# First table's inputs and constants on SP's queue, and a new written order up to the second block's gate tiles, in an S4 convolution with a gated layer

## The chip, the cores and the metric

The kernel runs on one core of a Trainium2 chip. The core has a matrix engine (TensorE, PE in the profile, with PEld for its weight loads), a vector engine (DVE), a scalar engine for function tables (ACT), GpSimd (POOL) and a sync engine (SP) that here only issues DMAs. Every engine works through its own instructions in program order and waits for others by semaphores. DMAs are issued by SP, ACT or POOL, each with a queue of its own, and are moved by 16 DMA engines. The metric is device time in microseconds, the median of several executions.

## The reference

An input x of 2048 tokens by 448 channels passes two blocks, each with a layer norm and a modulation from a small vector c:

```python
x = A_u
mod = (silu(c) @ w_mod)                      # six rows of 448: sa, ca, ga, sb, cb, gb
h = layernorm(x) * (1 + ca) + sa
x = x + ga * conv(h)                         # S4 convolution, per channel
h = layernorm(x) * (1 + cb) + sb
x = x + gb * ((gelu(h @ w_gate) * (h @ w_up)) @ w_down)
```

The convolution's kernel is `K[d, l] = Re sum_n C[d,n] * exp(dt[d] * A[d,n] * l) * dt[d] * B[d,n]` for 256 complex states n and 2048 positions l, with `dt = exp(log_dt)`. `conv(h)` is the causal convolution of each channel of h with K (by FFTs of length 4096 in the reference) plus `h * Dskip`. The inner width of the gated layer is 1792.

## The kernel before, in words

The kernel is a list of 2006 tasks. Each has a name and a function that emits a few instructions; `PLACE` (lines 40 to 263) holds, for every name, one number for each of its tasks, and the tasks are emitted in the order of these numbers. A letter behind a number chooses the engine where there is a choice: a for ACT, d for DVE, p for POOL, s for SP. Since every engine runs its instructions in program order, `PLACE` is the order by which each engine and each DMA queue works. Costs that stand in the `add` calls are not read when the kernel is built.

**Start and tables.** The states' parameters come in four tables of 112 channels (`abc`, the function `prep`). For a table, two loads `p.ld` bring C, B and A; A1 and A2 form C times B on DVE; S1 to S4 on ACT and B1, D1, G1, E1 on DVE turn it into a log magnitude and a phase; C1, C2 and A3 scale A by dt. The results are cut into bf16 pieces: c0, d0, e0, f0 for the magnitudes, c1, d1, e1, f1 for the phases. `p.put0` and `p.put1` store them to the DRAM buffer `lh_d`, into which `pad` also copies two constant rows, and `lt0` and `lt1` load them back, transposed by the access pattern, as weights of matmuls, for 7 groups of 8 channels at a time. dt itself is made by the task `dt` from `c.ld`, and `silu` and `sil2` prepare c for the modulation.

Before the change the first table's two loads are issued by ACT, its pad by POOL, and everything else of the start by SP, beginning with a block of x (`x.ld`), which is followed by log_dt, c, and three blocks of w_mod (`m.ld`).

**Table phase.** For each of 56 groups of channels, PE makes exponents and angles (`x.mm`, `y.mm`, `ang`, `anc`) out of the weights and the constant tables `ea` and `rd` (`c.ea`, `c.rd`); ACT turns them into exponentials and sines (`x.exp`, `y.exp`, `sin`, `cos`), for some with an absolute value first (`mag`); DVE multiplies (`tx`, `tyc`); PE sums over the states (`kgen`). Two groups at a time, the result is taken out of PSUM (`kev`), gets Dskip (`kd`), is transformed by PE over 32 positions (`ka`) and copied out (`kout`).

Beside it the input is normed (`bn`, `norm`, and `as`, which scales a constant matrix by the tokens' deviation), transformed (`ua`, taken out by `ua.ev`, stored by `ua.st`) and brought to frequencies (`ub`, `ub.ev`, `ub.eg`, `ub.st`). For the channels up to 320, `f.fwd`, `f.pr`, `f.inv`, `f.z` and `f.st` transform K further, multiply by the input's spectrum, transform back and store the result `y`.

**Tail transforms.** The last 128 channels go through `t.fwd`, the products `t.p0` and `t.p1`, and two inverse transforms: `t.i0` for the rows that the first token block needs, through `t.z0`, a store `t.s0` to `yb_d` and loads `yi.l0` and `yi.l1`, and `t.inv` for the others, through `t.z` and `t.st`. The matrices come by `t.fc` (first part) and `t.fd` (second part, which only `t.inv` needs).

**Gated layer.** `co.mme` and `co.mml` sum the convolution's output for the first of four blocks of 512 tokens; residual and norm follow on DVE and ACT; `co.ta` and `co.tb` transpose the columns on PE. The gate and up matmuls (`gu2` in two halves for the first four tiles, then `gu`) and the down matmuls run block by block. The weights are split into f16 pairs on the chip (`w.le`, `w.la`, `w.ld` load them; `w.hi`, `w.lo`). `co.mmx`, a y load `yi.ld` and DMA transposes prepare the next block meanwhile.

How a task's number and letter become program order:

```python
        at = PLACE[n][i]
        self.at, e = int(at.rstrip("adps")), at[-1]
        self.on = {"a": "ACT", "d": "DVE", "p": "POOL", "s": "SP"}.get(e) or next(iter(eng))
...
        out = sorted(self.tasks, key=lambda t: t.at)
```

Lines of the profile: 511 and 514 are the first table's loads and pads, 542 is A1, 595 the stores of the pieces, 620 the loads of the weights, 638, 657 and 675 the exponent and angle matmuls, 721 and 725 the products, 748 `kgen`, 771 `ka`, 480 and 482 copies on ACT and DVE by a helper, 852 the loads of x, 805 those of w_mod, 1138 and 1140 `t.fc` and `t.fd`, 1189, 1207 and 1216 the tail's matmuls, 1224 and 1297 the stores and loads of `yb_d`, 1332 the weight loads, 1409 `co.mml`, 1470 the transposes, 1524 and 1530 the gate and up matmuls.

## Time and profile before

| | |
|---|---|
| median of 3 runs | 787.2 us (786.79 to 788.53) |
| the profiled execution, its own time | 788.84 us |
| its span, first to last instruction | 787.0 us |
| time outside the span | 1.84 us |
| PE busy | 728.1 us |
| DVE busy | 591.6 us |
| ACT busy | 459.5 us |
| moved by DMA | 139.87 MB |
| mean granted TensorE clock | 0.991 |

A row of the timeline has the start, the length, the engine, the line, the operation with its output and input, the count, and in brackets the idle time before it with what ended it. "SPq" and "ACTq" rows are DMAs being issued, not moved. A row of the groups has the count and, behind the bar, the busy time and the mean of one in ns, then the idle time of the engine ahead of them. A row of the stretches has the busy time of PE, PEld, DVE, ACT and POOL, the granted clock of TensorE, the busy share of the DMA engines and what they moved in GB/s. A row of the DMA issues ends with the size and the median time from issue to landing.

### The profile page before, as it was taken

The page shows a single profiled execution, that of the slowest core. Times are in us where ns is not written, and L with a number is a line of the kernel's source. Part 1 is how long each engine was busy: PE and PEld are TensorE (multiplying, and loading weights), DVE is VectorE, ACT ScalarE, POOL GpSimd, SP SyncE. Part 2 cuts the span into 40 slices and gives each one's busy share as a digit, 9 for nine tenths or more (in the row PEclk, how much of TensorE's full clock was granted, in tenths as well). Part 3 has the DMA queues.
Part 4 walks back from the last instruction along what each step waited for, and adds up shares of the span by engine and source line. Part 5 has one row for each costly group of instructions (what it writes and reads, how often), then busy time and mean ns, then how long its engine had stood idle before and what let it go on. Part 6 is the DMA issues. An engine that isn't in the chain of part 4 may idle for free.

```text
span 787.0 us, 19037 instructions
## 1 busy us (share of the span) xinstructions
PE 728.1 (93%) x8166; PEld 443.6 (56%) x8166; DVE 591.6 (75%) x893; ACT 459.5 (58%) x611; POOL 9.0 (1%) x24
## 2 busy tenths in 40 slices
PE   1786889998899999989999999999999999999998
PEld 0333454543667767768784445444595446944478
DVE  5989999999999999988768851469773587133743
ACT  4799999899999999961555640233421244012320
POOL 0000000000000000000300000000000000000000
PEclk9989899999999999999999999999999999999999
DMA  9654458997878767999697875345447324012201
GB/s 260 180 162 141 142 148 242 298 263 225 255 232 223 222 190 212 290 294 252 193 311 231 273 191 159 129 129 188 164 67 206 111 94 134 14 47 94 82 2 59
DMA packets 103790, 139.87 MB, mean 178 GB/s; under 512 B 34388, under 2 KB 85268, under 8 KB 103706
## 3 DMA queue, kind: packets, MB, share of 16 engines
q1 hardware_dynamic: 99940, 131.61, 57.0%
q10 hardware_dynamic: 3206, 6.07, 2.3%
q8 instruction: 64, 1.05, 0.6%
q0 software_dynamic: 560, 0.98, 0.4%
q14 instruction: 20, 0.16, 0.1%
HBM read 100.39 MB, written 36.01 MB: 173 GB/s over the span
## 4 chain that ended last, share of the span: by engine, by line
PE 69%; DVE 4%; ACT 4%; DMA 2%; issue 2%; SPq 1%; DVEq 0%; ACTq 0%
PE pq L1530 31%; PE pq L1630 9%; PE pf L1105 4%; PE pd L1599 4%; PE kg L748 4%; PE pf L1094 3%; PE pg L675 2%; PE pq L1524 2%; PE kg L771 2%; PE pd L1630 2%; DVE ty L725 1%; PE pd L1404 1%; PE pg L657 1%; ACT fg L692 1%; PE pf L1189 1%
## 5 line engine op out<-in xcount | busy, mean ns | idle before, releaser
L1530 PE MATMUL pq<-ht,wr 128*128 128x512 f16 (+1 forms) x1200 | 248.5, 365 | 1.3 <-DMA ht<-hl 1.2
L1530 PEld LDWEIGHTS <-wr 128*128 128x128 f16 x1200 | 114.5, 98 | 130.0 <-issue 13.0
L725 DVE TENSOR_TENSOR ty<-my,fg 128x2048 f32<-128x2048 f32 x56 | 127.5, 2283 | 0.8 <-issue 0.5
L1537 ACT ACTIVATE ge<-pq 128x512 f32<-128x512 f32 (+1 forms) x60 | 33.9, 565 | 102.1 <-PE pq L1524 68.7
L1544 DVE TENSOR_TENSOR fq<-ge,pq 128x512 f32<-128x512 f32 (+1 forms) x60 | 38.9, 649 | 71.5 <-PE pq L1530 44.3
L1556 ACT ACTIVATE hh<-fq 128x1024 f16<-128x1024 f32 (+1 forms) x49 | 46.7, 961 | 64.9 <-DVE fq L1544 46.4
L721 DVE TENSOR_TENSOR tx<-mx,fg 128x1024 f32<-128x1024 f32 x56 | 67.7, 1218 | 2.4 <-ACT fg L692 1.0
L1630 PE MATMUL pq<-d,hh 128*128 128x224 f16 x476 | 68.9, 259 | 0.0
L748 PE MATMUL kg<-ty,tx 128*32 128x64 f32 x3584 | 63.6, 222 | 4.7 <-issue 2.6
L748 PEld LDWEIGHTS kg<-ty,tx 128*32 128x32 f32 x3584 | 53.8, 111 | 23.8 <-issue 15.7
L1559 DVE TENSOR_TENSOR hlo<-fq,hh 128x1024 f16<-128x1024 f32 (+1 forms) x49 | 53.7, 1106 | 12.9 <-ACT hh L1556 12.7
L1630 PE MATMUL pq<-d,hlo 128*128 128x224 f16 x238 | 61.6, 259 | 0.0
L688 ACT ACTIVATE fg<-pg 128x1024 f32<-128x1024 f32 x56 | 58.0, 1038 | 1.2 <-PE pg L675 0.8
L662 ACT ACTIVATE my<-pg 128x1024 f32<-128x1024 f32 x56 | 55.5, 1031 | 2.0 <-PE pg L657 1.9
L1630 PEld LDWEIGHTS <-hh 128*128 128x128 f16 x560 | 54.1, 98 | 0.9 <-issue 0.2
L1105 PE MATMUL pf<-q,fc 128*128 128x160 f32 x264 | 41.5, 307 | 1.1 <-DVE q L1098 1.1
L692 ACT ACTIVATE fg<-fg,small 128x1024 f32<-128x1024 f32 x36 | 41.5, 1170 | 0.1
L1747 ACT ACTIVATE d<-fq 128x896 f16<-128x896 f32 x14 | 13.3, 947 | 46.1 <-PE pd L1599 27.3
L1105 PEld LDWEIGHTS pf<-q,fc 128*128 128x128 f32 x264 | 36.4, 190 | 6.5 <-issue 1.5
L675 PEld LDWEIGHTS <-lt 64*128 64x128 bf16 x304 | 18.0, 96 | 38.8 <-issue 26.5
L675 PE MATMUL pg<-ea,lt 64*128 64x512 bf16 x152 | 30.5, 392 | 7.6 <-ACT fg L699 3.4
L984 PE MATMUL pf<-ui,fu 128*128 128x448 f32 x66 | 31.0, 575 | 1.6 <-ACT uo L480 1.4
(210 smaller groups left out, 1117.6 us busy)
## 6 DMA issues: line engine op xcount, KB each, us to landing
wr<-w_d SPq DMA_DIRECT2D x21, 896.0 KB, 5.2
fc<-in_k_fc SPq DMA_DIRECT2D x20, 576.0 KB, 3.7
u_d<-so SPq DMA_DIRECT2D x32, 224.0 KB, 2.8
ui<-u_d SPq DMA_DIRECT2D x10, 672.0 KB
fq<-in_wd SPq DMA_DIRECT2D x14, 448.0 KB, 6.1
w<-in_wgu SPq DMA_DIRECT2D x11, 512.0 KB, 7.4
us<-uo SPq DMA_DIRECT2D x22, 240.0 KB, 5.2
q<-us SPq DMA_DIRECT2D x22, 240.0 KB, 6.4
```

What stands on the lines that cost most here:

```text
L662: A.activation(yb.tile.rearrange("p h (n k) -> p n h k", n=2), pb.tile.rearrange("p (n h k) -> p n h k", n=2, h=2), AF.Exp)
L675: T.matmul(pa[:, nh * 512:nh * 512 + 512], w, x, start=(k == 0), stop=(k == 2))
L688: A.activation(fb.tile[:, 0].rearrange("p x (n k) -> p n x k", n=2), pb.tile.rearrange("p (n x k) -> p n x k", n=2, x=2), AF.Sin, scale=TW ...
L692: A.activation(fb.tile[:, 1], fb.tile[:, 1], AF.Sin, scale=-TWO_PI, bias=halfpi)
L721: V.tensor_mul(tx.tile, xb.tile[:, xm, None, :].to_broadcast([128, 2, 512]), fb.tile[:, :, 0])
L725: V.tensor_mul(ty.tile, yb.tile[:, :, None, :].to_broadcast([128, 2, 2, 512]), fb.tile[:, None, :, 1].to_broadcast([128, 2, 2, 512]))
L748: T.matmul(kg[32 * g:32 * g + 32, 2 * (s % 2) + q, :64], tx[:, r, nh, 4 * q + g], ty[:, 0:4:3, nh, 4 * q + g] if r else ty[:, 1:3, nh, 4 * ...
L1105: T.matmul(pz.tile[:, e % 32 - sl0], fc.tile[:, i, 1 + t], pp.tile[:, t, i], start=(t == 0 and e != 32), stop=(t == 1 and e != 0))
L1530: T.matmul(pb.tile[k][:, ts], wr.tile[:, 4 * lo + t, k, c0:c0 + 128], ht[:, m, ts], start=f % 2 == 0 and i == 0, stop=f % 2 == 1 and i == 9)
L1556: A.activation(hg.tile[0][:, cb, c], fq.tile[:, c], AF.Copy)
L1559: V.tensor_sub(hg.tile[1][:, cb, c], fq.tile[:, c], hg.tile[0][:, cb, c])
L1630: T.matmul(bank(k)[:, m], x[:, p, q[0], ts], w[:, p, q[1]], start=new and m == 0 and p == 0 and z == 0, skip_group_check=True, stop=i in ( ...
```

## The change

Two things are changed. In `prep`, the two loads and the pad of the first table are issued by SP, as those of the other three tables were; ACT and POOL issue no DMA in the start any more. And `PLACE` has new numbers (and in part new letters) for every task up to number 1480; from there on all numbers are as before. The first table's first load is number 0 on SP, then come a block of x, the second load, c, a block of w_mod, log_dt, two more blocks of w_mod with a block of x between them, the pad, and the store of the first pieces. Some names have other letters. No task is added or removed. Of the table's rows only those that the text speaks of are shown.

```diff
--- before.py
+++ after.py
@@ -38,49 +38,49 @@
...
-    "as": "66d 64d 79d 107d 116d 151d 119d 185a 250d 258d 265a 289d 309d 333d 334d 365d",
+    "as": "69a 58a 101d 98d 121d 126d 174a 167d 251d 255a 280d 289a 311d 324d 334d 353a",
...
-    "c.c": "21",
+    "c.c": "16",
...
-    "c.ld": "11",
+    "c.ld": "21",
...
-    "c.rd": "58",
+    "c.rd": "78",
...
-    "co.ta": "1401 1406 1453 1436",
+    "co.ta": "1404 1410 1432 1434",
...
-    "co.tb": "1411 1413 1454 1439",
+    "co.tb": "1407 1414 1443 1446",
...
-    "dt": "12",
+    "dt": "24",
...
-    "f.fwd": "738 753 783 806 832 855 879 902 924 947 969 998 1014 1036 1055 1077 1098 1120 1141 1162 1209 1216",
+    "f.fwd": "727 759 786 809 821 850 884 892 930 950 966 998 1015 1028 1056 1075 1095 1120 1136 1160 1206 1218",
...
-    "f.z": "758a 778d 802a 829a 868a 871d 896d 926a 952d 979a 1005d 1019a 1038d 1061a 1085a 1102a 1128d 1143a 1163a 1188a "
-        "1235a 1239a",
+    "f.z": "755a 772d 812d 832a 865a 887d 908d 928a 949a 986d 993d 1009d 1027d 1066d 1085a 1098d 1111a 1132a 1155a 1183a "
+        "1219a 1233d",
...
-    "gu2": "1420 1427 1442 1457 1464 1467 1470 1473",
+    "gu2": "1422 1423 1442 1457 1459 1464 1471 1472",
...
-    "kev": "191d 238d 285d 351d 368d 401d 431d 497a 551d 579d 661a 680d 737d 786a 816a 856a 890d 922a 948d 980d 1045d 1065a "
-        "1104d 1146a 1183d 1198a 1219a 1246a",
+    "kev": "218d 224a 290d 317a 373d 394d 448a 490a 548d 569d 699d 707d 735d 806d 797d 858a 900a 918a 960d 975a 1037a 1071d "
+        "1101a 1138a 1166a 1195a 1235a 1238d",
...
-    "kout": "247a 288a 318a 377d 448a 414a 505a 530a 583d 634d 720d 733d 771a 811a 843a 892d 928a 962a 992a 993d 1076a 1110d "
-        "1142a 1177a 1200a 1228a 1251d 1252a",
+    "kout": "229a 266a 299d 342a 442d 407a 507a 544a 658a 598a 710a 738d 739a 843a 804a 877d 917a 945d 976a 994a 1070d 1094a "
+        "1130a 1167a 1188a 1211a 1244d 1246a",
...
-    "lt0": "65 149 317 358 568 766 860 955",
+    "lt0": "61 112 302 369 561 744 852 1017",
...
-    "lt1": "103 150 335 393 696 833 971 995",
+    "lt1": "95 162 384 432 742 745 965 1060",
...
-    "m.cp": "532d 589a 818d",
+    "m.cp": "553a 604a 793d",
...
-    "m.ld": "24 32 23 423 539 727",
+    "m.ld": "27 36 17 433 558 761",
...
-    "p.A3": "25 174 435 618",
+    "p.A3": "25 154 346 487",
...
-    "p.C1": "13 92 422 543",
+    "p.C1": "28 102 420 500",
...
-    "p.C2": "18 113 427 552",
+    "p.C2": "32 103 421 607",
...
-    "p.E1": "38 169 437 644",
+    "p.E1": "38 171 446 639",
...
-    "p.G1": "19 117 434 571",
+    "p.G1": "35 128 436 615",
...
-    "p.S1": "14 100 328 547",
+    "p.S1": "5 104 331 542",
...
-    "p.S2": "16 112 364 569",
+    "p.S2": "8 114 366 565",
...
-    "p.S3": "27 133 410 588",
+    "p.S3": "9 125 390 579",
...
-    "p.c0": "31a 194d 439a 662a",
+    "p.c0": "26a 159d 428d 632d",
...
-    "p.c1": "43d 183d 471a 682d",
+    "p.c1": "44a 241d 511a 729d",
...
-    "p.e1": "53a 217a 481a 692d",
+    "p.e1": "56d 321a 584d 845d",
...
-    "p.f0": "36 242 460 704",
+    "p.f0": "40 244 459 730",
...
-    "p.ld": "3 5 70 91 168 291 490 507",
+    "p.ld": "0 7 86 87 170 265 368 452",
...
-    "p.put0": "48 281 464 837",
+    "p.put0": "49 301 475 814",
...
-    "pad": "4 203 278 785",
+    "pad": "48 247 181 695",
...
-    "silu": "22",
+    "silu": "18",
...
-    "t.fd": "1256 1231 1244 1274 1221 1237 1215 1234",
+    "t.fd": "1180 1242 1266 1322 1227 1382 1376 1375",
...
-    "t.i0": "1269 1297 1296 1300 1310 1307 1314 1318 1334",
+    "t.i0": "1267 1274 1278 1307 1301 1311 1314 1331 1326",
...
-    "t.inv": "1272 1282 1290 1326 1354 1362 1376 1386 1395",
+    "t.inv": "1262 1315 1291 1350 1348 1359 1361 1406 1398",
...
-    "t.s0": "1315s 1304s 1309s 1313s 1319s 1330a 1322a 1333a 1342s",
+    "t.s0": "1300s 1318s 1289s 1310s 1309s 1319a 1320a 1336a 1328s",
...
-    "t.z0": "1280a 1301a 1298a 1305a 1316a 1311a 1320a 1324d 1337a",
+    "t.z0": "1273a 1297a 1288a 1308a 1306a 1312a 1316a 1332a 1327a",
...
-    "ua.ev": "78d 83a 88a 93d 110d 111d 120d 123d 141a 144a 156a 166d 188a 192d 231a 211a 259a 261a 267a 268a 299a 296a 303a "
-        "310d 325a 331a 344d 340a 366a 367d 375d 380d",
+    "ua.ev": "76d 74d 84d 88d 115d 111d 134d 130d 137a 148a 153a 155d 192d 185a 207a 215d 258a 256a 267a 270a 288a 284a 298a "
+        "305a 328a 329a 343d 336a 364d 362d 367d 372a",
...
-    "w.le": "1285 1344 1323",
+    "w.le": "1304 1290 1351",
...
-    "x.ld": "46 8 201 154",
+    "x.ld": "33 4 226 156",
...
-    "yi.l0": "1361s 1332s 1340p 1353p 1365s 1363p 1343p 1357p 1370p",
+    "yi.l0": "1369s 1360s 1335p 1367p 1345s 1337p 1354p 1371p 1368p",
...
-    "yi.l1": "1352s 1331p 1338a 1367p 1348s 1360p 1350p 1358s 1368s",
+    "yi.l1": "1357s 1373p 1313a 1365p 1358s 1340p 1362p 1372s 1363s",
...
@@ -508,12 +508,12 @@
         def ld1(i):
             if i == 0:
                 b1.tile = pq.tile([DT, 4, N], FT, name="q")
-            (dma if t else adma)(b3.tile[:, :2] if i else b1.tile, a["abc"][t, :, 4:] if i else a["abc"][t, :, :4])
-
-        L0 = add("p.ld", {"SP" if t else "ACT": 0.42 if t else 0.1}, v0, lambda: ld1(0), (), [b1], (), kb=459)
-        PAD[t] = add("pad", {"SP": 0.7} if t else {"POOL": 1.0}, v0 + 0.5, lambda: (dma if t else P.dma_start)(lh_d[t, :, :, 6:], a["k_one"][t]), [L0], kb=300)
+            dma(b3.tile[:, :2] if i else b1.tile, a["abc"][t, :, 4:] if i else a["abc"][t, :, :4])
+
+        L0 = add("p.ld", {"SP": 0.42}, v0, lambda: ld1(0), (), [b1], (), kb=459)
+        PAD[t] = add("pad", {"SP": 0.7}, v0 + 0.5, lambda: dma(lh_d[t, :, :, 6:], a["k_one"][t]), [L0], kb=300)
         L3 = add("p.al", {"NONE": 0.0}, v0, al3, (), [b3])
-        L1 = add("p.ld", {"SP" if t else "ACT": 0.42 if t else 0.1}, v0, lambda: ld1(1), [L0, L3], (), [b3], kb=230)
+        L1 = add("p.ld", {"SP": 0.42}, v0, lambda: ld1(1), [L0, L3], (), [b3], kb=230)
 
         def op(n, e, fn, deps, table=None, alloc=(), use=(), k=0.0):
             return add("p." + n, e, v0 + dv * k, fn, deps, alloc, [b for b in us if b not in alloc] + list(use), table=table)
```

248 rows, old and new, of the table PLACE are left out of this document.

## The prediction

> **What bounds the kernel now.** I read the totals first, then the busy time by stage, because one list of engine shares mixes stages with different limits. The stretches are the start, the table phase, the tail transforms, the entry to the gated layer, the first gate tiles, and the rest.
>
> ```profile
> span 787.0 us, 19037 instructions
> ...
> 0.00:28.00 28.00, 11.27 (x26) 4.54 (x26) 17.88 (x44) 13.78 (x24) 1.51 (x11) 1.00 0.83 233
> 28.00:352.00 324.00, 289.23 (x5233) 181.22 (x5236) 309.68 (x375) 305.75 (x378) 0.00 (x0) 0.98 0.74 219
> 352.00:375.00 23.00, 21.99 (x304) 19.24 (x293) 19.05 (x32) 4.04 (x12) 1.56 (x3) 1.00 0.94 256
> 375.00:393.00 18.00, 16.30 (x148) 12.99 (x141) 13.77 (x33) 10.74 (x21) 5.27 (x10) 1.00 0.69 191
> 393.00:464.00 71.00, 69.95 (x442) 37.97 (x439) 55.70 (x97) 40.55 (x62) 0.69 (x1) 1.00 0.82 249
> 464.00:787.00 323.00, 319.35 (x2038) 187.63 (x2038) 175.54 (x314) 84.63 (x118) 0.00 (x0) 1.00 0.37 110
> ```
>
> After the length of the stretch stand PE, PEld, DVE, ACT and POOL busy, the granted clock, the DMA share and GB/s. From 393 us on PE is busy 389.3 of 394 us, and the change leaves every place after 1480 (the second block's gate tiles) alone. So the run ends as much earlier as the first gate tile starts earlier, unless something behind it then lacks data. In the table phase DVE (309.7 of 324) and ACT (305.8) set the pace together: DVE has 14.3 us of idle time there. In the start, DVE is idle for 10.1 us. The next view is the start in order of time.
>
> ```profile
> 0.74 0.91 ACTq L511 DMA_DIRECT2D q<-in_abc  x2
> ...
> 0.75 0.41 SPq L852 DMA_DIRECT2D xt<-in_A_u  x1
> ...
> 7.87 1.23 DVE L542 TENSOR_TENSOR q<-q 112x1024 f32<-112x1024 f32 x1 [6.96 <-DMA q<-in_abc]
> ...
> 9.47 0.42 DVE L548 TENSOR_TENSOR q<-q 112x256 f32<-112x256 f32 x1
> 9.53 0.20 ACT L494 ACTIVATE dts__106<-ld 112x4 f32<-112x4 f32 x1 [6.56 <-DMA ld<-in_A_log_dt]
> ...
> 10.86 0.61 ACT L551 ACTIVATE q<-q 112x512 f32<-112x512 f32 x1
> ...
> 21.92 0.31 SPq L595 DMA_DIRECT2D lh_d<-lh  x1
> ...
> 24.95 1.35 SPq L620 DMA_DIRECT2D lt<-lh_d  x2
> ...
> 28.40 0.28 PE L638 MATMUL pg<-rd,lt 64*128 64x256 bf16 x1 [0.69 <-DMA lt<-lh_d]
> ```
>
> This is one chain: the first table's inputs land, the first product starts at 7.87, steps of DVE and ACT in turn follow, the first half goes out (21.92, 14.05 us after the product), comes back as matmul weights (24.95, 3.03 later), and the first table matmul runs at 28.40 (3.45 later).
>
> **The change, part by part.** *First inputs.* They are issued at the same 0.74, but on SP's queue, with the 896 KB of x behind them instead of beside them.
>
> ```profile
> q<-in_abc ACTq DMA_DIRECT2D x1, 448.0 KB, 7.1
> ...
> fc<-in_k_fc SPq DMA_DIRECT2D x20, 576.0 KB, 3.7
> ...
> 2.00:4.00 2.00, 0.00 (x0) 0.00 (x0) 0.00 (x0) 0.96 (x1) 0.28 (x1) 1.00 0.74 254
> ```
>
> 448 KB took 7.1 us from issue to landing. 576 KB on SP's queue typically took 3.7, so the product could start at 0.75 + 3.7 = 4.45; the late bound is today's 7.87. The DMA engines move 0.5 MB between 2 and 4 us, near what this load needs. I take 4.6, by the nearer row: 3.3 us earlier. [...]
>
> *The chain behind it.* Squares now follow the parts at once (they waited from 9.89 to 10.86 behind dt's and the turn's instructions: 0.97 less), and Exp no longer stands behind A3 (0.4 less). Against that C2, G1 and E1 now stand ahead of the last subtraction f0: 0.39, 0.43 and two like the 0.42 of L585, 1.66 more. So the output is issued 14.05 − 1.37 + 1.66 = 14.3 after the product: 18.9 instead of 21.92, 3.0 earlier. SP's queue is the next thing that could be late, since x, three loads of w_mod and now the pad are ahead of it, the same bytes as today.
>
> ```profile
> 13.33 0.39 DVE L567 SCALAR_TENSOR_TENSOR q<-q 112x256 f32<-112x256 f32 x1
> 13.76 0.43 DVE L582 SCALAR_TENSOR_TENSOR q<-q 112x256 f32<-112x256 f32 x1
> ...
> 15.67 0.49 ACT L561 ACTIVATE q<-q,dts__106 112x256 f32<-112x256 f32 x1
> ...
> 21.76 0.42 DVE L585 SCALAR_TENSOR_TENSOR q<-q 112x256 f32<-112x256 f32 x1
> ...
> 20.00:22.00 2.00, 2.00 (x4) 0.77 (x4) 1.93 (x5) 0.42 (x1) 0.00 (x0) 1.00 0.02 7
> ```
>
> The queues are empty from about 20 us (share 0.02 from there to 22). An output issued at 18.9 finds up to 1.1 us of data ahead, inside the 3.03 us that its landing takes anyway. I count 0.1 for it: the first table matmul comes **2.9 us** earlier. The constants rd and ea stay behind the output; ea, now ahead of the load of the table, moves while SP waits for the landing. If the load lands no earlier than today, the term is 0; at most it is 7.87 − 4.45 − 0.28 = 3.1. Issuing the first pad from SP costs it some 0.4 us, while it is waiting for f0.
>
> *Engines.* Counting the letters in the two lists, DVE loses 4 of the scaled matrices, 3 ke, 2 ako and one zo of 448 (priced like so, its size), and gets 4 zo, 2 so and 3 lh (net).
>
> ```profile
> L482 DVE COPY so<-pf 128x448 f32<-128x448 f32 x13 | 7.9, 617 | 0.8 <-PE pf L921 0.7
> ...
> L482 DVE COPY ke<-kg 128x252 f32<-128x252 f32 x17 | 7.0, 410 | 0.6 <-PE kg L748 0.4
> L482 DVE COPY ako<-kg 128x512 f32<-128x512 f32 x9 | 6.1, 683 | 1.3 <-PE kg L771 1.3
> ...
> L911 DVE TENSOR_SCALAR as<-au,rs 128x128 f32<-128x128 f32 x14 | 3.8, 280 | 2.1 <-PE pf L921 2.1
> ...
> L482 DVE CAST lh<-q 112x512 bf16<-112x512 f32 x8 | 3.3, 417 | 0.1
> L482 DVE COPY zo<-pf 128x480 f32<-128x480 f32 x7 | 4.6, 652 | 0.5 <-PE pf L1105 0.5
> ```
>
> Out: 4 × 0.28 + 3 × 0.41 + 2 × 0.68 + 0.62 = 4.3. In: 4 × 0.65 + 2 × 0.62 + 3 × 0.42 = 5.1. DVE gets 0.8 us more. Up to 1.06 of it, the last zo (f.z[21]) and the last ke, now stands behind the last table product, where DVE waits for PE. Work ahead of that product is about even: 0. ACT does a little less.
>
> *The middle order.* No operation and no byte of the table phase changes, only who goes first. What can change is DVE's idle time, 14.3 us.
>
> ```profile
> 100.00:150.00 50.00, 46.01 (x838) 23.81 (x835) 49.33 (x62) 45.89 (x63) 0.00 (x0) 1.00 0.77 216
> 150.00:200.00 50.00, 43.65 (x646) 20.47 (x644) 47.16 (x64) 49.06 (x63) 0.00 (x0) 1.00 0.89 258
> ```
>
> A good stretch loses 0.67 in 50 us, a poor one 2.84. Over 324 us that is 4.3 or 18.4: from 10.0 us less to 4.1 us more. I see no wait that is plainly added or removed. Two that I followed: lt1[4] moves on SP's queue from ahead of ub.st[10], f.ut[0] and f.fc[0] to behind them, right before the angle matmuls that read it, and f.fwd[0] comes earlier, behind its two loads. ACT has exponentials to do meanwhile. I take 0.
>
> *The tail.* The yb_d stores and loads set the start of the gated layer.
>
> ```profile
> 372.59 1.99 PE L1207 MATMUL pf<-q,fg 128*96 128x128 f32 x16
> ...
> 392.57 2.34 PE pq L1530 x20
> ```
>
> In the new order one large inverse transform fewer stands on PE ahead of the last two t.i0, and the last z0 leaves by ACT's queue. One such transform is 1.99 us, so this is worth 0 to 2.0; DVE's t.p products, as many as before, feed the same steps, and I take half, 1.0. Against it t.inv[7] now stands between the first two transposes co.ta[0] and co.tb[0], ahead of gu2[0] (392.57): 0 to 2.0, and I take 0.7, since the split of the second column group runs meanwhile. Together **0.3** earlier, from 2.0 earlier to 2.0 later.
>
> Sum: 2.9 + 0 + 0 + 0.3 = **3.2 us**. The profiled execution took 788.84 us, 1.84 outside its span; made against it, it would take 785.6. The median of the three runs is 1.64 lower, 787.2, and with the same 3.2 us I predict **784.0 us**.
>
> **The rivals.** *The early start is lost again in the first stretch with a slow PE clock.*
>
> ```profile
> 38.00:42.00 4.00, 4.00 (x18) 1.55 (x18) 2.79 (x9) 3.51 (x4) 0.00 (x0) 0.50 0.18 66
> 42.00:44.00 2.00, 2.00 (x12) 0.75 (x9) 0.41 (x2) 1.94 (x2) 0.00 (x0) 0.62 0.00 0
> ```
>
> Here the clock is 0.50 and DVE is idle 1.21 + 1.59 = 2.8 us behind ua's matmuls. PE starts its work earlier in the new order, with as thin a load behind it; a second such stretch would cost 2.8, and the time would be 786.8. For it: PE is busy only 11.27 of the first 28 us. Against: the same work gave one such stretch today, and nothing in the new order asks for two. Without any, the time would be 784.0 − 2.8 = 781.2. [...]
>
> *The tail gets slower (the other side).* The second matrices t.fd[5], [6] and [7] move from 1215-1237, ahead of the early y load, to 1375-1382, behind the last of seven yb_d loads on SP, and t.fd[5] also behind a store that waits for z. t.inv[8] (1398) and t.inv[7] (1406) need them and stand on PE ahead of co.tb[0] (1407) and gu2[0] (1422).
>
> ```profile
> my<-in_k_ft SPq DMA_DIRECT2D x6, 192.0 KB, 5.9
> ...
> xt<-in_A_u SPq DMA_DIRECT2D x4, 896.0 KB, 13.1
> ...
> 376.41 6.24 SPq L1297 DMA_DIRECT2D yi<-yb_d  x6
> ```
>
> In today's times the last yb_d load leaves SP at 382.65, t.fd[5] about 0.9 later at 383.5 (three issues); with 5.9 us it lands at 389.4, t.inv[7] (1.99) ends at 391.4, and gu2 can still start about when it does. It decides above some 6 us. With 13.1, the slowest row of this queue, gu2 starts 7.2 us later: 784.0 + 7.2 = 791.2. For it: the DMA share from 352 to 375 is 0.94. Against: these are 192 KB, and in 375 to 393 the share is 0.69. One more us of landing is one more us of time, so the time passes 788.8 at 10.7 us.
>
> *The change doesn't bring the inputs earlier* because the first load's time is issue and receipt, not sharing: then 7.1 us stays, the longer chain costs 0.3, and the tail gives it back: 787.2.
>
> **How the numbers follow.** The forecast, 784.0, has 0.58; its own range is 781.5 to 785.5. The fast end, no slow clock or less idle time in the middle, to 780, has 0.08. No gain (the lost start or the unmoved inputs), 785.6 to 788.8, has 0.18. The slow tail, or up to 4.1 us more idle time in the middle, has 0.16, and reaches from 788.8 to 791.2. What a measurement can tell from no change is 0.2%, 1.6 us: faster means under 785.6, slower above 788.8. Faster: 0.58 + 0.08 = 0.66; same 0.18; slower 0.16. The range leaves out less than half of each end: 780.0 to 789.5.
>
> **What would show it.** The first DVE product before 5.5 us and the first table matmul before 26.5 show the start right; a product after 7 shows it wrong. In the table phase DVE's busy time should be within 1 us of 327.6 up to the last product, and its idle time from the first matmul to the last product near 14. The first gate matmuls should start about 389.4, and from there to the end it should take the same 394.4 us. If t.inv[7] waits for a DMA, the rival of the tail is at work; a clock of 0.50 in more than one stretch with DVE idle shows the other. I am wrong if DVE's idle time in the middle moves by more than 3 us.

## The result and the profile after

The changed kernel takes 783.19 us (median of 6 runs, 781.91 to 785.97) against 787.87 (6 runs, 786.62 to 791.25) for the kernel before: ratio 0.9942, 95% interval 0.9920 to 0.9963. The forecast was 784.0, with a range of 780.0 to 789.5. The profiled execution took 783.97 us, 4.87 less than the one of before.

The start in order of time, from the timeline of the changed kernel (start, duration, engine, line, what it does, and in brackets the idle time before and who ended it):

```profile
0.75 0.41 SPq L511 DMA_DIRECT2D q<-in_abc  x1
...
4.91 1.22 DVE L542 TENSOR_TENSOR q<-q 112x1024 f32<-112x1024 f32 x1 [4.00 <-DMA q<-in_abc]
...
6.96 0.63 ACT L551 ACTIVATE q<-q 112x512 f32<-112x512 f32 x1 [0.72 <-DVE q L548]
...
12.12 0.51 ACT L577 ACTIVATE q<-q,ld 112x256 f32<-112x256 f32 x1
...
19.05 0.33 SPq L595 DMA_DIRECT2D lh_d<-lh  x1
...
21.99 1.35 SPq L620 DMA_DIRECT2D lt<-lh_d  x2
...
25.13 0.39 PE L657 MATMUL pg<-ea,lt 64*128 64x512 bf16 x1 [0.65 <-DMA lt<-lh_d]
```

The first product starts at 4.91 instead of 7.87, the first output leaves at 19.05 instead of 21.92, and the first table matmul runs at 25.13 instead of 28.40. Square (L551) now follows the product's parts at once, at 6.96 instead of 10.86.

Then the busy time by stretch, cut at the same events in both kernels: the first table matmul, the last two groups at L771 and, for the changed kernel, the first gate matmul (columns as in the prediction). The kernel before, up to the end of the table phase:

```profile
0.00:28.40 28.40, 11.27 (x27) 4.55 (x27) 18.23 (x45) 14.18 (x24) 1.51 (x11) 1.00 0.83 231
28.40:352.24 323.84, 289.47 (x5238) 181.36 (x5240) 309.33 (x373) 305.35 (x377) 0.00 (x0) 0.98 0.74 219
```

The changed kernel:

```profile
span 782.0 us, 19039 instructions
...
0.00:25.13 25.13, 10.99 (x26) 4.38 (x27) 18.46 (x47) 14.51 (x26) 0.87 (x10) 1.00 0.80 248
25.13:346.75 321.62, 289.56 (x5238) 181.54 (x5240) 308.56 (x370) 303.85 (x377) 0.00 (x0) 0.98 0.78 222
346.75:369.00 22.25, 20.89 (x277) 17.62 (x278) 18.99 (x32) 5.76 (x15) 0.70 (x1) 1.00 0.79 239
369.00:387.40 18.40, 16.65 (x149) 13.91 (x146) 13.57 (x33) 9.45 (x18) 6.12 (x11) 1.00 0.84 252
387.40:458.00 70.60, 70.36 (x445) 38.44 (x444) 55.04 (x94) 41.02 (x64) 0.69 (x1) 1.00 0.77 239
458.00:782.00 324.00, 319.75 (x2040) 187.71 (x2038) 176.11 (x315) 84.95 (x118) 0.00 (x0) 1.00 0.36 109
```

So 3.27 us were won in the start (28.40 to 25.13) and 2.22 more in the table phase (323.84 to 321.62). There DVE works 0.77 less (309.33 to 308.56) and is idle 1.45 less (14.51 to 13.06). The first gate matmul comes 5.19 earlier (392.57 to 387.38), so the tail gave 0.30 back, and from there to the end it takes 394.6 us instead of 394.4. DVE's work up to the last groups at L771 is 327.0 in all, against 327.6.

The tail in PE's timeline of the kernel before:

```profile
385.11 0.66 PE L1409 MATMUL pd<-yi,ai 128*64 128x128 f32 x8 [1.11 <-DMA yi<-yb_d]
...
386.14 1.04 PE L1207 MATMUL pf<-my,fg 128*96 128x128 f32 x8
387.01 2.78 PE L1207 MATMUL pf<-my 128*96 128x128 f32 x24
```

and of the changed kernel:

```profile
378.85 0.44 PE L1409 MATMUL pd<-yi,ai 128*64 128x128 f32 x4 [1.23 <-DMA y<-lh]
...
383.14 0.39 PE L1470 MATMUL pd<-idenh,hl 128*128 128x128 f16 x4
383.37 1.07 PE L1207 MATMUL pf<-my,fg 128*96 128x128 f32 x8
384.27 1.04 PE L1207 MATMUL pf<-my 128*96 128x128 f32 x8
385.14 0.39 PE L1470 MATMUL pd<-idenh,hl 128*128 128x128 f16 x4
386.04 0.38 PE L1470 MATMUL pd<-idenh,hl 128*128 128x128 f16 x4 [0.51 <-DVE ht L482]
```

The late products (L1409) start at 378.85 instead of 385.11, 6.26 earlier. From there to the first gate matmul it takes 8.53 instead of 7.46. t.inv[7] stands between the transposes (383.37 to 385.3), as forecast. It is no added work there: in the kernel before, t.inv[7] and t.inv[8] both stand behind the late products too, ahead of the first transpose (386.14 to 389.8). The third transpose waits for DVE's eviction of ht.

### The profile page after: what moved, and what is told of

The parts are those of the page before. It is cut to its first block, busy times and chain, and to the rows that moved or that the text cites. A ratio compares the mean times of both kernels' runs of the same rounds, so it can differ in the third digit from the quotient of the medians.

```text
span 782.0 us, 19039 instructions
## 1 busy us (share of the span) xinstructions
PE 728.2 (93%) x8166; PEld 443.6 (57%) x8166; DVE 590.7 (76%) x889; ACT 459.6 (59%) x615; POOL 8.4 (1%) x23
## 3 DMA queue, kind: packets, MB, share of 16 engines
q8 instruction: 64, 1.05, 0.6%
## 4 chain that ended last, share of the span: by engine, by line
PE 66%; ACT 9%; DMA 8%; DVE 7%; issue 3%; SPq 2%; ACTq 0%; POOL 0%; DVEq 0%; POOLq 0%
PE pq L1530 24%; PE pq L1630 9%; PE pf L1105 5%; PE pg L675 4%; PE kg L748 4%; PE pd L1599 4%; PE pf L1094 3%; PE kg L771 2%; DMA w<-in_wgu 2%; PE pq L1524 2%; PE pd L1630 2%; ACT fg L688 1%; ACT my L662 1%; PE pf L984 1%; DVE ty L725 1%
## 5 line engine op out<-in xcount | busy, mean ns | idle before, releaser
L1530 PE MATMUL pq<-ht,wr 128*128 128x512 f16 (+1 forms) x1200 | 248.5, 365 | 0.4 <-DMA ht<-hl 0.4
L1530 PEld LDWEIGHTS <-wr 128*128 128x128 f16 x1200 | 114.5, 98 | 128.5 <-issue 11.8
L725 DVE TENSOR_TENSOR ty<-my,fg 128x2048 f32<-128x2048 f32 x56 | 127.6, 2281 | 0.0
L1544 DVE TENSOR_TENSOR fq<-ge,pq 128x512 f32<-128x512 f32 (+1 forms) x60 | 38.9, 649 | 72.3 <-PE pq L1530 44.3
L721 DVE TENSOR_TENSOR tx<-mx,fg 128x1024 f32<-128x1024 f32 x56 | 67.8, 1216 | 4.4 <-ACT fg L692 3.0
L748 PEld LDWEIGHTS kg<-ty,tx 128*32 128x32 f32 x3584 | 52.8, 110 | 21.6 <-issue 13.4
L748 PE MATMUL kg<-ty,tx 128*32 128x64 f32 x3584 | 61.5, 220 | 3.5 <-issue 1.6
L1559 DVE TENSOR_TENSOR hlo<-fq,hh 128x1024 f16<-128x1024 f32 (+1 forms) x49 | 53.7, 1106 | 13.4 <-ACT hh L1556 13.3
L688 ACT ACTIVATE fg<-pg 128x1024 f32<-128x1024 f32 x56 | 57.8, 1037 | 2.1 <-DVE tx L721 2.0
L1105 PE MATMUL pf<-q,fc 128*128 128x160 f32 x264 | 43.4, 314 | 1.0 <-DVE q L1098 0.7
L680 ACT ACTIVATE fg<-pg 128x1024 f32<-128x1024 f32 x30 | 31.1, 1037 | 2.0 <-PE pg L675 1.7
```

What stands on the lines that cost most here:

```text
L688: A.activation(fb.tile[:, 0].rearrange("p x (n k) -> p n x k", n=2), pb.tile.rearrange("p (n x k) -> p n x k", n=2, x=2), AF.Sin, scale=TW ...
L721: V.tensor_mul(tx.tile, xb.tile[:, xm, None, :].to_broadcast([128, 2, 512]), fb.tile[:, :, 0])
L725: V.tensor_mul(ty.tile, yb.tile[:, :, None, :].to_broadcast([128, 2, 2, 512]), fb.tile[:, None, :, 1].to_broadcast([128, 2, 2, 512]))
L748: T.matmul(kg[32 * g:32 * g + 32, 2 * (s % 2) + q, :64], tx[:, r, nh, 4 * q + g], ty[:, 0:4:3, nh, 4 * q + g] if r else ty[:, 1:3, nh, 4 * ...
L1105: T.matmul(pz.tile[:, e % 32 - sl0], fc.tile[:, i, 1 + t], pp.tile[:, t, i], start=(t == 0 and e != 32), stop=(t == 1 and e != 0))
L1530: T.matmul(pb.tile[k][:, ts], wr.tile[:, 4 * lo + t, k, c0:c0 + 128], ht[:, m, ts], start=f % 2 == 0 and i == 0, stop=f % 2 == 1 and i == 9)
```

## The experiments

The executions of one kernel differ by some 3 to 10 us, and a ratio below, from 4 to 12 of them, has an interval of 0.002 to 0.003 to each side. Each kernel left one profile; the one with the inputs alone left two. The ratios are against the kernel before, run beside it on the same chip. "Table" is the start of the first table matmul, "last" the end of DVE's last product at L725 (one at L721 follows it and ends 1.1 us later), "gate" the first matmul at L1530.

| kernel | first product | table | last | gate | ratio (95%) | mean clock |
|---|---|---|---|---|---|---|
| before | 7.87 | 28.40 | 349.94 | 392.57 | 1 | 0.988 |
| changed | 4.91 | 25.13 | 344.46 | 387.38 | 0.9942 (0.9920, 0.9963) | 0.992 |
| inputs alone | 4.91 | 28.78 | 351.08 | 393.39 | 0.9972 (0.9953, 0.9991) | 0.988 |
| the same, second profile | 4.58 | 26.52 | 345.28 | 387.84 | one run | |
| inputs and Square | 4.65 | 26.27 | 349.63 | 391.90 | 0.9993 (0.9969, 1.0017) | 0.989 |
| start alone | 4.71 | 26.17 | 345.08 | 387.20 | 0.9966 (0.9946, 0.9986) | 0.988 |
| order alone | 7.67 | 27.83 | 348.55 | 391.87 | 0.9981 (0.9958, 1.0004) | 0.990 |
| new middle, old tail | 4.84 | 24.89 | 343.62 | 387.98 | 0.9935 (0.9911, 0.9959) | 0.992 |
| t.inv[7] late | 4.79 | 27.14 | 345.35 | 388.44 | 0.9944 (0.9925, 0.9964) | 0.994 |
| transposes as before | 4.83 | 25.22 | 341.69 | 383.68 | 0.9936 (0.9911, 0.9962) | 0.994 |
| small loads early | 4.55 | 25.60 | 345.80 | 387.97 | 0.9969 (0.9947, 0.9991) | 0.992 |
| 64 small matmuls at the start | 8.18 | 28.77 | 347.91 | 391.22 | 1.0022 (1.0000, 1.0044) | 0.988 |
| 16 pairs of bf16 matmuls | 7.74 | 28.22 | 354.93 | 401.21 | 1.0101 (1.0070, 1.0133) | 0.988 |
| 14 f32 matmuls | 7.39 | 28.03 | 355.98 | 401.89 | 1.0130 (1.0097, 1.0164) | 0.993 |

### Inputs alone, twice

```diff
 order of the kernel before, with ld1 and pad as in the change
-ACT: p.ld[0], p.ld[1]    POOL: pad[0]
+SP: p.ld[0], x.ld[1], p.ld[1], c.ld, c.c, m.ld, x.ld[0], pad[0], p.put0[0]
```

> The old order of everything, but the first table's two loads and its pad on SP's queue, the first load ahead of all. Theory (the early start carries through to the end): first product at 4.9 instead of 7.87, first table matmul near 25.4 instead of 28.40, first gate matmuls 3.0 earlier than 392.57, near 389.5, time 3.0 under the kernel before, near 784.9 against 787.9. Rival (the start is lost again in the first stretch with thin work on PE and a slow clock): first table matmul near 25.4 all the same, but DVE's idle time from there to the last product grows from 13.4 to about 16, and the time is 787 or more.

> The same kernel as with the inputs alone, for a second profile, since its first was the slowest of its twelve executions. Theory: the small load ld lands near 9 to 10 again, Square starts near 10.5 to 11.3, first table matmul 28.0 to 28.8. Rival (that profile was an outlier and the small load is usually early): Square before 9.5, first table matmul before 27.

The product came early both times and the first table matmul did not follow as expected. ACT's rows of the first profile:

```profile
9.94 0.20 ACT L494 ACTIVATE dts__106<-ld 112x4 f32<-112x4 f32 x1 [7.92 <-DMA ld<-in_A_log_dt]
...
11.28 0.61 ACT L551 ACTIVATE q<-q 112x512 f32<-112x512 f32 x1
```

and of the second:

```profile
7.69 0.20 ACT L494 ACTIVATE dts__106<-ld 112x4 f32<-112x4 f32 x1 [5.66 <-DMA ld<-in_A_log_dt]
...
9.02 0.61 ACT L551 ACTIVATE q<-q 112x512 f32<-112x512 f32 x1
```

Square stands behind dt's two instructions, and these wait for ld, a load of 112x4 numbers. It landed at 9.94 once and at 7.69 once, with the same program. So the theory of an early load that carries through by itself fell at the first table matmul. Its worth there is what the small load allows: nothing (28.78) or 1.88 us (26.52 against 28.40). The second profile meets the rival's terms, Square before 9.5 and the table matmul before 27; which of the two is the usual case, two profiles can't say. Over its twelve executions the kernel is 2.2 us faster than the one before (0.7 to 3.7), where 3.0 were forecast.

### Inputs and Square, start alone, order alone

```diff
 inputs and Square: as inputs alone, and
-ACT: dt, C1, S1, S2      DVE: A1, A2, bn[4], bn[6], B1
+ACT: S1, S2, dt, C1      DVE: A1, A2, B1, bn[4], bn[6]
```
```diff
 start alone: the 66 steps up to lt0[0] in the new order, all behind them in the old one
 order alone: the whole new order, but
-SP: p.ld[0], p.ld[1], pad[0]
+ACT: p.ld[0], p.ld[1]    POOL: pad[0]
```

> The kernel with the inputs alone moved (old order otherwise), and in the first table's chain only S1 (Square and Abs), B1 and S2 (Ln) put right behind A2, ahead of dt's two instructions on ACT and of the first statistics of x on DVE. Theory (the early load is worth nothing while Square stands in ACT's queue behind dt's instructions, which wait for the small load ld, and worth some 3 us once it doesn't): Square at 6.9 instead of 11.28, first table matmul near 25.8 instead of 28.78, time 2 to 3 under the kernel before. Rival (other steps of the old order hold the chain): first table matmul 27.5 or later.

> The new order only for what stood ahead of the first load of the table (66 steps: the inputs on SP's queue, the first table's chain with Square ahead of dt's instructions), the old order for all the rest. Theory (the early load and the new order of ACT's first instructions are both needed, and together they carry to the end): first product 4.9, first table matmul near 25.1 (28.40 before), first gate tiles 3.3 earlier than before, near 389.3, time 3.3 under the kernel before. Against the run with the inputs alone (first product 4.91, first table matmul 28.78) this shows that ACT's order was the other half. Rival (the start is absorbed by waits in the middle): first table matmul near 25.1, and the time less than 1.5 under the kernel before.

> The new order of everything, but the first table's two loads on ACT's queue and its pad on POOL's as before. Theory (the start is due to the inputs, the middle to the order, and the two add up): first product back at 7.9, first table matmul near 28.1, time 3.0 above the changed kernel's 783.2, near 786.2. Rival (the order makes the gain and the queue of the inputs makes no difference to the end): 783 to 784.

With Square ahead of dt the table matmul came at 26.27 and 26.17, and with the order but the load at 7.67 it came at 27.83, 0.57 earlier than before. So at the first table matmul the new order of ACT makes the early load's gain sure, and is worth little without the early load. Start alone missed the 25.1 expected there, because its first table matmul waited 1.92 for the load of rd, which the old order has behind. The times don't separate the two. Start alone is 2.7 us faster than the kernel before (1.1 to 4.3; 3.3 forecast). With inputs and Square the forecast of 2 to 3 us failed: 0.5 faster, −1.3 to 2.4. In its profile the 2.1 us of the start were gone at the last product (349.63 against 349.94), with 15.3 us of DVE idle time in between instead of 13.4; that is the rival of the lost start, in one profile. Order alone came out as forecast, 3.1 us above the changed kernel by the ratios.

Six profiles with the early load and the whole new start (the changed one, start alone, the three of the tail below, and small loads early) have the table matmul at 24.89 to 27.14, 25.7 in the mean; four with neither have 28.03 to 28.77, 28.4 in the mean. The start is worth 2.7 us at that point. The late one of the six, 27.14, is t.inv[7] late, whose program up to there is the changed kernel's; its small load was late:

```profile
13.30 0.51 ACT L577 ACTIVATE q<-q,ld 112x256 f32<-112x256 f32 x1 [1.22 <-DMA ld<-in_A_log_dt]
```

How much of it reaches the end: the three kernels with an early load and the old middle have ratios of 0.9972, 0.9993 and 0.9966, in the mean 0.9977, 1.8 us. The five with the new middle as well have 0.9942, 0.9935, 0.9944, 0.9969 and 0.9936, in the mean 0.9945, 4.3 us. So the rest of the new order is worth about 2.5 us by these means, which order alone (1.5 us in all, 0.57 of it in the start) shows less clearly. The profiles agree in the mean and overlap: from the first table matmul to the last product ("table" to "last") it takes 318.8 to 323.4 us in six with the old middle (320.7 in the mean; the two with matmuls added at 30 to 46 us are left out), and 316.5 to 320.7 in the six with the new one (318.9 in the mean).

### Small loads early

```diff
-SP: p.ld[0], x.ld[1], p.ld[1], c.c, m.ld[2], c.ld, ...
+SP: p.ld[0], c.ld, c.c, x.ld[1], p.ld[1], m.ld[2], ...
```

> The changed kernel with the two small loads ld and c (issued at 3.18 and 2.15 on SP's queue) right behind the first input load, ahead of x and of w_mod. Theory (once the first input is early, the small load ld is the next thing that is late on ACT's queue: it let L577 start at 12.12 in the changed kernel, and at 13.30, after a wait of 1.22, in the run with t.inv[7] behind gu2[1], whose start is the same program): L577 without a wait at 12.1 or earlier, first table matmul at 24.9 or earlier, time 0 to 1.2 under the changed kernel's 783.2. Rival (the small load waits for bandwidth and not for its place in the queue): it lands no earlier, the same 25.1 to 27.1.

L577 started at 11.77 without a wait, as expected, but the first output took longer to land (issue of the table's load 3.68 after it, 2.94 in the changed kernel), and the table matmul came at 25.60, not 24.9; nor is the time (0.9969) under the changed kernel's. The small load's place is not what the changed kernel lacks; a single profile can't say whether it removes the late case of 13.30.

### The tail

```diff
 new middle, old tail: the new order up to ka[27], the old one behind it
 t.inv[7] late:
-PE: t.inv[8], co.ta[0], t.inv[7], co.tb[0], co.ta[1], co.tb[1], co.mml[2], gu2[0], gu2[1]
+PE: t.inv[8], co.ta[0], co.tb[0], co.ta[1], co.tb[1], co.mml[2], gu2[0], gu2[1], t.inv[7]
 transposes as before:
+PE: t.inv[8], co.ta[0], co.ta[1], co.mml[2], co.tb[0], co.tb[1], gu2[0], gu2[1], t.inv[7]
```

> The changed kernel up to the last critical matmuls of the table phase, and behind them the order of the kernel before. Theory (the new tail costs 0.4 us in all: 0.8 won up to the late products, 1.1 lost from there to the first gate tiles): from the last two groups at L771 to the first gate matmuls 40.3 us as before instead of 40.7, time 0.4 under the changed kernel's 783.2, near 782.8. Rival (the new tail is worth what was forecast, 0.3): 41.0, time near 783.5. If the middle's gain of 2.2 is chance and not the new order, the last product comes more than 1 us later than 344.5.

> The changed kernel with the inverse transform t.inv[7] moved from between the first two transposes co.ta[0] and co.tb[0] to behind the second gate tile gu2[1], its eviction and store with it. Theory (t.inv[7] stands on the path there and costs 1.1): from the first matmul at L1409 to the first at L1530 7.5 us instead of 8.6, and the whole 1.1 earlier, near 782.1. Rival (PE has to do it anyway, and behind the gate tiles it costs what it saved): 7.5 too, but from the first gate matmul to the end 395.6 instead of 394.5, and the time stays at 783.2.

> The changed kernel with the transposes of the first two row blocks in the order of the kernel before (co.ta[0], co.ta[1], the products co.mml[2], then co.tb[0], co.tb[1]) and t.inv[7] behind gu2[1]. Theory (the 1.1 us lost between the late products and the first gate tile come from DVE's eviction co.cb[0], which stands behind the second row block's split on DVE while co.ta[1] waits for it, and hardly from t.inv[7], whose move alone brought 8.53 to 8.31): from the first matmul at L1409 to the first at L1530 about 7.0 to 7.5 us instead of 8.5, time 0 to 1.0 under 783.2, since the 2.0 of t.inv[7] are paid behind the gate tiles if PE has no idle time there. Rival (PE's total work sets it): 7.5 there and 395.6 behind it, time 783.2.

With the old tail it takes 42.1 us from the last groups at L771 to the first gate matmul, where 40.3 were forecast and 41.0 by the rival; neither holds. In that profile the late products started only at 380.53, behind a wait of 2.86 for the last part of y, and the time (0.9935) is that of the changed kernel. Moving t.inv[7] alone brought 8.53 to 8.31 from the late products to the first gate matmul: 0.22, not 1.1. The transposes in the old order as well brought it to 7.31. PE's rows of that kernel:

```profile
376.37 0.44 PE L1409 MATMUL pd<-yi,ai 128*64 128x128 f32 x4 [1.63 <-DMA y<-lh]
...
380.72 0.40 PE L1470 MATMUL pd<-idenh,hl 128*128 128x128 f16 x4
382.09 0.40 PE L1470 MATMUL pd<-idenh,hl 128*128 128x128 f16 x4 [0.98 <-ACT hl L480]
...
383.68 0.60 PE L1530 MATMUL pq<-ht,wr 128*128 128x256 f16 x4
```

What is left of the loss goes with the wait for DVE's eviction of the transposed block, 0.51 in the changed kernel's row at 386.04 and 0.84 with t.inv[7] late; DVE does it behind the second row block's split. The old order of the transposes with t.inv[7] left in place wasn't run, so the shares of the two are not separated. Yet nothing came of removing it: from the late products to the end it is 403.3 us here (779.7 − 376.37), 403.15 in the changed kernel (782.0 − 378.85) and 403.9 with t.inv[7] late. PE does t.inv[7] behind the first gate tiles instead, and from the first gate matmul to the end takes 395.5 and 396.0 instead of 394.6. The rival was right, and the three ratios, 0.9935 to 0.9944, are those of the changed kernel. No kernel here beats it by more than the interval.

### Added work on PE: the clock, and a surprise

```diff
 16 pairs of bf16 matmuls; 14 f32 matmuls: the kernel before, with products that nothing uses
+PE, between 30 and 46 us: T.matmul(hot, ea[:64, :128], rd[:64, :512])   16 x 2
+PE, between 31 and 46 us: T.matmul(hot[:, :256], au, gs1[:, :256])      14 x 1
 64 small matmuls at the start: the kernel before, and ahead of all else on PE
+T.matmul(hot[:1, :1], eps, eps)                                          64 x 1
```

> The kernel before with 16 pairs of matmuls into an unused PSUM tile (about 0.43 us a pair at full clock) put between PE's instructions of the first stretch, 30 to 46 us; the extra products are used by nothing. Theory (DVE's 2.8 us of idle time from 38 to 44 come from the half clock there, not from the order of work): the stretch of 6.8 us at 0.50 from 36.7 is gone or shorter, DVE's idle time from the first table matmul to the last product falls from 13.4 to about 10.6 to 11.5, time 2 to 2.8 under the kernel before. Rival (the waits are those of the order, or the added work costs as much as the clock): idle time 13 to 16, time the same or up to 3 more.

> The kernel before with 14 f32 matmuls of 128x256 (about 0.5 us each at full clock) into an unused PSUM tile, put between PE's instructions from 31 to 46 us; 14 instructions more instead of 64. Theory (the first slow stretch of 6.8 us cost DVE some 1 us, not the 2.8 of idle time that stand in it, and there is no stall near 126): no half clock before 50 us, DVE's idle time from the first table matmul to the last product 12 to 13.4, time 0 to 1.5 under the kernel before. Rival (the slow stretch costs the whole 2.8): idle 10.6, time 2.5 or more under it.

> The kernel before with 64 matmuls of 1x1 at the very start of PE's program, where PE has nothing to do until 16 us; they are used by nothing. Theory (the 5 us in which PE issued nothing near 124 to 129 in the run with added matmuls came from the place of the boundaries between PE's 16 KB blocks of instructions, which 64 more instructions move by a quarter of a block into a stretch of full DMA queues): again a wait of 3 to 7 us of PE without a releaser near 120 to 130, time 3 to 8 over the kernel before. Rival (the stall came from the added work, or by chance): no such wait, the time of the kernel before within 1.5 us.

The f32 matmuls did what they should to the clock. The kernel before and the one with 14 f32 matmuls, by stretch:

```profile
30.00:40.00 10.00, 6.54 (x30) 2.65 (x32) 9.16 (x20) 9.74 (x15) 0.00 (x0) 0.83 0.57 164
40.00:50.00 10.00, 7.95 (x68) 3.45 (x68) 7.89 (x13) 9.30 (x10) 0.00 (x0) 0.82 0.32 94
50.00:120.00 70.00, 56.05 (x1074) 30.63 (x1062) 67.83 (x97) 68.18 (x88) 0.00 (x0) 0.95 0.56 160
```

```profile
30.00:40.00 10.00, 9.94 (x44) 4.09 (x44) 8.93 (x20) 9.27 (x14) 0.00 (x0) 1.00 0.55 159
40.00:50.00 10.00, 9.62 (x53) 3.61 (x53) 7.11 (x12) 8.26 (x10) 0.00 (x0) 1.00 0.31 94
50.00:120.00 70.00, 54.55 (x1088) 30.63 (x1087) 68.52 (x98) 69.53 (x89) 0.00 (x0) 1.00 0.57 158
```

The granted clock is 1.00 throughout instead of 0.82 to 0.95, and DVE's idle time from 30 to 120 is 5.4 us against 5.1. So the full clock did not give back the 2.8 us; the added matmuls, 0.70 us each in the timeline, may hide a smaller gain. With the bf16 pairs the stretch at 36.7 is gone as well, two of 3.4 us stay (62.9 and 76.6), and DVE's idle time from 30 to 120 is 3.7. What the half clock costs there stays open. Both expectations fell: DVE's idle time to the last product is 18.9 and 19.8 us, not 10.6 to 13.4, and the kernels are slower, by 1.0% and 1.3%. The largest part of that starts at one place, here in the kernel with 14 f32 matmuls:

```profile
124.73 1.09 PE L748 MATMUL kg<-ty,tx 128*32 128x64 f32 x62
129.71 0.30 PE L748 MATMUL kg<-ty,tx 128*32 128x64 f32 x2 [3.88 <-issue]
129.94 4.09 PE L984 MATMUL pf<-ui,fu 128*128 128x448 f32 x6
```

In the middle of a group of 64 matmuls PE stops for 3.88 us, and the profile shows nothing that it waits for. With the bf16 pairs (lines are shifted by 13 there) it stops in the same group, four matmuls earlier:

```profile
123.26 1.08 PE L761 MATMUL kg<-ty,tx 128*32 128x64 f32 x58
129.31 0.43 PE L761 MATMUL kg<-ty,tx 128*32 128x64 f32 x6 [4.98 <-issue]
```

The same place in the kernel before:

```profile
124.53 1.10 PE L748 MATMUL kg<-ty,tx 128*32 128x64 f32 x64
125.56 2.81 PE L984 MATMUL pf<-ui,fu 128*128 128x448 f32 x6
```

The instruction queue shows what goes with it. PE's program comes in blocks of 16 KB: queue q8 ("instruction") of the kernel before has 64 packets with 1.05 MB, 16 KB each, and 65 with 64 matmuls more on PE (both rows stand below). The DMA view of the kernel with 14 f32 matmuls, from 120 to 127 us and from 127 to 128.4:

```profile
q1 hardware_dynamic: 1135, 1.90, 86.1%
```

```profile
q1 hardware_dynamic: 44, 0.21, 50.1%
q8 instruction: 1, 0.02, 5.2%
```

No block moves while 1.9 MB of loads do; one moves as these end, and PE goes on 1.4 us behind it. That the stop is a boundary in PE's instructions can be counted. The rows up to 127 us with the bf16 pairs and with the f32 matmuls:

```profile
0.00:127.00 127.00, 89.79 (x1368) 47.57 (x1368) 111.20 (x182) 111.46 (x148) 1.51 (x11) 0.97 0.64 180
```

```profile
0.00:127.00 127.00, 90.91 (x1368) 46.48 (x1368) 111.34 (x182) 110.12 (x146) 1.51 (x11) 1.00 0.62 178
```

Both stop behind 1368 matmuls and 1368 weight loads, 2736 rows, at two places of the program: the pairs have added 64 rows there, and the 14 f32 matmuls, each of two matmul and two weight-load rows, 56. The kernel before has a block at 127.6 too, but PE comes to row 2736 only at 131.6, behind the long f32 matmuls of L984, and doesn't run dry. Stops without a releaser come at other boundaries as well, in the kernel before and in the changed one:

```profile
338.03 0.42 PE L748 MATMUL kg<-ty,tx 128*32 128x64 f32 x14 [1.25 <-issue]
```

```profile
325.13 0.75 PE L748 MATMUL kg<-ty,tx 128*32 128x64 f32 x36 [1.55 <-issue]
```

These are behind row 9865 and row 9612, 253 rows apart, close to the 255 that the 64 blocks and 16332 rows of the kernel before give for one block. Inputs alone, inputs and Square, start alone and the 14 f32 matmuls stop at row 9865 too, for 1.2 to 1.9 us, and new middle, old tail and t.inv[7] late at row 9612. In each case PE goes on 1.2 to 1.6 us after a block has landed.

The run with 64 small matmuls was meant to move a boundary with nothing else, and showed no such wait near 125; it is 1.7 us slower than the kernel before (0 to 3.5). Its queue tells why. The kernel before and it:

```profile
q8 instruction: 64, 1.05, 0.6%
```

```profile
q8 instruction: 65, 1.06, 0.6%
```

It added one whole block (128 matmul and 128 weight-load rows), so all boundaries stayed where they were in the program (the packets of the blocks behind the added one start at 48.9, 59.2 and 63.9 us, those of the kernel before at 49.0, 59.4 and 64.4; with the bf16 pairs at 38.9, 55.3 and 62.8). The expected quarter of a block was wrong. So the counts show that PE stops at a boundary; that the loads in the queues hold the block back is inferred, since no run took them away. Up to 388 us, 44 blocks land in the kernel before and 44 in the changed one; stops of over 0.5 us without a releaser, 1.4 to 1.6 us behind a landed block, are two in the first (1.25 and 0.91 us) and one in the second (1.55), against 3.88 and 4.98 in the two runs above.

## Why the prediction was right, step by step

**Start, 2.9 forecast: right, 3.27 in the profile and 2.7 in the mean.** The product came 2.96 earlier (3.3 forecast), the chain behind it took 14.14 (14.3), the output's landing cost nothing more. The product starts at 4.55 to 4.91 with the load on SP's queue and at 7.39 to 8.18 with it on ACT's, beside x. The queues from 2 to 5 us, before and after:

```profile
q1 hardware_dynamic: 72, 0.52, 49.8%
q10 hardware_dynamic: 77, 0.32, 34.2%
```

```profile
q1 hardware_dynamic: 190, 0.94, 91.1%
```

Before, SP's queue (q1, with x) moved 0.52 MB while ACT's (q10) moved 0.32, less than the first load's 0.46; after, SP's alone moved 0.94, with the load ahead. So in these two traces its time was sharing, and the rival that the change doesn't bring the inputs earlier is out. What the step didn't see is that its 0.97 for Square isn't an extra. Without Square ahead of dt, the early load gave 0 and 1.88 at the first table matmul in two profiles.

**Engines, 0: right.** DVE's work up to the last groups at L771 fell by 0.6 (327.6 to 327.0), within the 1 us named. Up to the last product itself it fell by 0.9 (327.5 to 326.6), where the step had it about even; a last zo and ke now stand behind that product.

**The middle order, 0 taken, range −10.0 to +4.1: the mis-sized term.** It measured −2.2 in the profile and about −2.5 by the runs. Between the first table matmul and the last product DVE works 1.2 less in the profile (309.25 to 308.09; 0.2 of it is now done in the start, the rest mostly behind that product) and is idle 1.1 less (13.43 to 12.37). Only the second is what the step was about. Part of it goes with the clock. The rival named one slow stretch more or less, with DVE idle behind it. The start was not lost: the changed kernel has three stretches at 0.50, of 3.4 us each (35.7, 199.6 and 325.9), the kernel before two of 6.8 (36.7 and 77.6). That thin work on PE brings such a stretch was the author's assumption, and the two traces bear it out in part: PE is busy for 1.37 to 1.70 us of the 3.4 ahead of each of the five, but also for only 1.15 of the 3.4 from 194.6 in the kernel before, where the clock is 1.00 and stays there. DVE is idle for 0.26, 1.13 and 0 us in the three stretches of the changed kernel, and for 2.71 and 0.04 in the two of the kernel before. The last of the three begins right behind PE's stop at a block boundary (325.13). Over all runs the new order has less slow time: a stretch that begins between 73 and 78 us stands in the six profiles with the old middle named above, and in none of the six with the new one; the mean granted clock is 0.992 to 0.994 with the early load and the new middle, 0.988 to 0.989 with the old middle. Within the runs of one kernel, 0.001 of mean clock goes with 0.42 us (standard error 0.05, 184 degrees of freedom), so 0.004 goes with 1.7. That is a correlation: a late load may make PE as idle as it is ahead of the five stretches, and so bring both the lower clock and the longer time. And the run that held the clock at 1.00 up to 120 us gained nothing there (the one with the bf16 pairs 1.4 us of idle time). What makes the 2.2 stays open.

**The tail, −0.3: near, +0.3, with one cause wrong.** Up to the late products it gave 0.77 (1.0 forecast; 6.26 less the 5.49 at the end of the table phase). Behind them it lost 1.07 (0.7 forecast for t.inv[7]). The forecast had t.inv[7] as added work, but it stood behind the late products before as well; moving it out gave 0.22, and the rest goes with the order of the transposes and DVE's eviction between them, so the 0.7 came near by luck. The rival on the other side did not come: t.inv[8] and t.inv[7] waited for no DMA.

**"The run ends as much earlier as the first gate tile starts earlier": not in general.** It held for the change (394.6 against 394.4), but with the transposes as before the gate tile came 3.70 earlier (383.68) and the end 2.3. Work of PE that is moved behind that start has to be paid there.

The sum was −3.2. The profiled execution gave −4.87, and the medians −4.68; nearly all of the difference is the middle.

## What to carry to other kernels

A load that comes earlier is worth what stands in each engine's order ahead of its consumer allows (here 0 and 1.88 us at the first table matmul, with a product 2.96 and 3.29 us earlier): look at that instruction, and at its own small load. Work moved off the path ahead of a saturated engine's start isn't gained if the same engine must do it behind (here 403.3 us from the late products to the end, against 403.15). And where an order of 2000 steps is searched anew, count slow-clock time over all runs, not in one profile: here single profiles of one program differ by more than the terms argued about.

## What the hardware showed unexpectedly

Fourteen added matmuls of 0.70 us, put where PE was partly idle, cost some 10 us. The largest part seen is that they moved the boundaries of PE's 16 KB instruction blocks in the program: PE stood still for 3.88 us behind row 2736, with 1.9 MB of loads in the queues, and for 2.10 us behind row 10629 in the tail (at 361.83), each time with no releaser in the profile. What became of the rest was not followed. In the run with bf16 pairs the clock was 0.50 for 6.8 us from 127.8 on. And a load of 112x4 numbers was waited for until 7.69 and 9.94 us in two profiles of one program, and until 13.30 in a third, issued at 2.1 and 3.1.
